# Attention, gated MLP, cosine MLP on one core: the order of both MLP layers written out by hand, with fixed leads for the weights

## The chip, the cores and the metric

The kernel runs on 1 core of a Trainium2 chip (trn2). Its engines are TensorE (PE), VectorE (DVE), ScalarE (ACT), GpSimd (POOL) and SyncE (SP), which here only issues DMAs. Each takes its instructions strictly in the order of its own list, and waits at an instruction whose inputs or buffers are not ready. The metric is device microseconds (us) of one launch, as the median of the runs.

## The reference, cut to what matters

```
attn[b,h] = softmax over keys in the query's hash bucket; out = attn @ v   # 2 x 8 heads, 768 x 64
x = attention out as 1536 tokens x 512
x = (sigmoid(x @ w_gate) * (x @ w_val)) @ w_out      # layer 1: 512 -> 1536 -> 512
h = x @ w_in                                          # layer 2: 512 -> 2048
y = (h * cos(h)) @ w_out2                             #          2048 -> 512
```

Weights arrive as float64, passed as pairs of 32-bit words.

## The kernel before, in words

Every fp32 product is made of three TensorE passes: each operand is split into a high part (rounded) and a low part (the rest), and high x high, high x low and low x high are added up in PSUM.

Attention comes first, in an order written out by hand. It writes its result, split, into `xy[c]`, where c = 0, 1, 2 are three groups of 512 tokens. The last heads finish c = 1 and c = 2.

The layers work in *items*. `("in", l, f, c)` is the first product of layer l for the f-th slice of 128 hidden columns and token group c: 24 matmuls of 512 columns in layer 1 (gate tile `pg` and value tile `pv`), 12 in layer 2 (`ph`). `("out", l, f, c)` multiplies the hidden slice into the output accumulators: 12 matmuls. Layer 1 has 12 slices and layer 2 has 16. For c = 0 the output item of a slice follows its three input items; those for c = 1 and c = 2 come in one long row at the end of the layer. So a *block* of layer 1 is 3 x 24 + 12 = 84 matmuls, one of layer 2 is 3 x 12 + 12 = 48, and layer 2 as a whole is 1152.

After an input item of layer 2 comes a chain that takes turns on two engines: ACT makes `n` (rounded phase), DVE makes `r`, ACT makes the sine in place in `r`, DVE makes `g`. Before the output item `g` has to be split by `gsplit`: ACT writes `gh`, DVE writes `gl`. In layer 1 the chain is a sigmoid on ACT and one product on DVE.

Each weight tile goes through three steps. `load_raw` puts 512 KB of float64 words into a `raw` buffer (SP queue). `convert` makes an fp32 tile `w_..`, of which there are 6 (`NEARLY`): `wp` on ACT, then `wl`, `wl`, `w` on DVE (L151 to L165). `wsplit` makes the high part on ACT (`ih`, `zh`, `gh`, `vh`, `oh`, L123) and the low part mostly on POOL (`il`, `zl`, ..., L124). The letters are g, v, o for layer 1 (gate, value, out) and i, z for layer 2 (in, out).

In both layers a scheduler decides the order on each engine before the kernel is built: it takes what is ready by its own estimate, with the order of the program as priority. The weights' three steps may therefore run far ahead, until the `raw` buffers (4) or the fp32 tiles (6) are full.

Of the kernel before, what the change touches and what calls it, by code (L numbers as in the profile page):

```python
# [9 lines left out]
F32 = mybir.dt.float32  # L10
# [29 lines left out]
def lsh_attention_glu_moe_cos_moe(  # L40
# [26 lines left out]

    const = ctx.enter_context(tc.tile_pool(name="const", bufs=1))

    wraw = ctx.enter_context(tc.tile_pool(name="wraw", bufs=4))  # L70
    NEARLY = 6

    ident = const.tile([P, P], F32, tag="ident", name="ident")
# [102 lines left out]


    def layer_items(l, F):
        items = [("in", l, 0, 0), ("in", l, 1, 0), ("in", l, 0, 1), ("in", l, 0, 2), ("in", l, 1, 1)]
        items += [("out", l, 0, 0), ("in", l, 1, 2), ("out", l, 1, 0)]  # L180
        for f in range(2, F):
            items += [("in", l, f, c) for c in range(NC)] + [("out", l, f, 0)]
        for f in range(F - 2):
            items += [("out", l, f, c) for c in range(1, NC)]
        items += [("out", l, f, c) for c in range(1, NC) for f in (F - 2, F - 1)]
        return items
# [7 lines left out]
            return [(nm, f, 0) for nm in ("gv" if l == 1 else "i")]  # L194
        return [("o" if l == 1 else "z", f, int(c > 0))]

    order = list(dict.fromkeys(kk for it in items for kk in weights_of(it)))
    done = 0
    def convert_to(n):
        nonlocal done  # L200
        while done < min(n, len(order)):
            load_to(done + 4)
            convert(order[done])
            done += 1

# [9 lines left out]
    def attention():  # L215
        with ExitStack() as st:
# [324 lines left out]
            with tc.manual_schedule(  # L541
                engines={
                    mybir.EngineType.PE,
                    mybir.EngineType.Activation,
                    mybir.EngineType.DVE,
                    mybir.EngineType.Pool,
                    mybir.EngineType.SP,
                }
            ):
                for t0 in (0, 3):  # L550
                    load(0, "q", t0, t0 + 3)
                    load(0, "k", t0, t0 + 3, eng=nc.scalar)
                constants()
                for g in range(2):
                    nc.sync.dma_start(pj[D * g : D * g + D, :], proj)
                nc.sync.dma_start(bcode, srow)
                load(1, "q")
                load(1, "k")
                load(0, "v")
                load(2, "k")  # L560
                load(2, "q")
                bit_weights()
                evac = [trans(0, half, fast=True) for half in range(2)]
                for fn in evac:
# [12 lines left out]
                coef(0)  # L577
                late.extend(bits(1, half) for half in range(2))
                for g in range(NG + LAG + 2):
                    wa, wb = 2 * (g - LAG), 2 * (g - LAG) + 1  # L580
                    fin = (wb - 2) // T if 0 <= wb - 2 < NW and (wb - 2) % T == T - 1 else None

                    def finish_group():
                        fin_act(fin)
                        if fin % 4 == 3:
                            at(g + SUM_AT, lambda u=fin: fin_sum(u))
                            at(g + HIGH_AT, lambda u=fin: fin_hi(u))
                            at(g + LOW_AT, lambda u=fin: fin_lo(u))

                    def early_weights():  # L590
                        if g == WL:
                            load_to(4)
                        if g in WC:
                            convert_to(1 + WC.index(g))
                            load_to(done + 4)

                    live_a, live_b, live_g = 0 <= wa < NW, 0 <= wb < NW, g < NG
                    ops = {
                        "PVb": (0 <= wb - 2 < NW, lambda: pv(wb - 2)),
                        "FIN": (fin is not None, finish_group),  # L600
                        "Tb": (live_b, lambda: ptrans(wb)),
                        "LOa": (live_a, lambda: plo(wa)),
                        "EXP": (live_g, lambda: expo(g)),
                        "PVa": (live_a and fin is None, lambda: pv(wa)),
                        "MIN": (g + 1 < NG, lambda: rowmax(g + 1)),
                        "HIb": (live_b, lambda: phi(wb)),
                        "Ta": (0 <= wa + 2 < NW, lambda: ptrans(wa + 2)),
                        "GRD": (live_g, lambda: guard(g)),
                        "COEF": (g + 1 < NG, lambda: coef(g + 1)),
                        "LOb": (live_b, lambda: plo(wb)),  # L610
                        "RCP": (live_g, lambda: recip(g)),
                        "NRM": (live_g, lambda: norm(g)),
                        "LATE": (True, run_late),
                        "W": (True, early_weights),
                        "S": (g + 2 < NG, lambda: scores(g + 2)),
                        "PVaF": (live_a and fin is not None, lambda: pv(wa)),
                        "PREP": (True, lambda: run_todo(g)),
                        "HIa": (0 <= wa + 2 < NW, lambda: phi(wa + 2)),
                    }
                    for name in ORDER if g >= LAG - 1 else FILL:  # L620
                        on, fn = ops[name]
                        if on:
                            fn()
                for step in sorted(todo):
                    run_todo(step)


    def moe():
        with ExitStack() as st:
# [8 lines left out]

            def wsplit(key):
                nm, f, again = key  # L640
                h = wsp.tile([P, KT, P], F32R, tag=ROLE[nm] + "h", name=f"{nm}h{again}_{f}")
                lw = wsp.tile([P, KT, P], F32R, tag=ROLE[nm] + "l", name=f"{nm}l{again}_{f}")
# [19 lines left out]
            gf, gs = {}, {}  # L662

            def gsplit(l, f, c):
                gh = wk.tile([P, 512], F32R, tag="gh", name=f"gh{l}_{c}_{f}", bufs=4)
                gl = wk.tile([P, 512], F32R, tag="gl", name=f"gl{l}_{c}_{f}", bufs=4)
                split(gh, gl, gf.pop((l, f, c)), nc.vector)
                gs[l, f, c] = gh, gl

# [8 lines left out]
                nc.vector.tensor_tensor(out=g, in0=pv_, in1=sg, op=ALU.mult)  # L678
                gf[1, f, c] = g

            def cos_in(c, f):
                ph = ps_h.tile([P, 512], F32, tag="h", name=f"ph{c}_{f}")
                proj_in(ph, c, ("i", f, 0))

# [4 lines left out]
                nc.vector.scalar_tensor_tensor(  # L689
                    out=r, in0=ph, scalar=INV2PI, in1=n, op0=ALU.mult, op1=ALU.subtract  # L690
                )
                nc.scalar.activation(r, r, AF.Sin, bias=halfpi, scale=TWOPI)
                g = gtile(2, f, c)
                nc.vector.tensor_tensor(out=g, in0=ph, in1=r, op=ALU.mult)
# [34 lines left out]
            def layer_out2(c, f):  # L729
# [3 lines left out]
                for t in range(4):  # L733
# [11 lines left out]
                        )  # L745
                        n += 1
                    if f == F2 - 1:
                        o = wk2.tile([P, 512], F32, tag="o", name=f"o{c}_{t}", bufs=3)
                        (nc.scalar.copy if t % 2 else nc.vector.tensor_copy)(o, acc[c, t])
                        b, tt = divmod(4 * c + t, T)  # L750
                        nc.sync.dma_start(
                            out.rearrange("(b p t) e -> b t p e", b=B, t=T)[b, tt], o
                        )


            ready = 0

            def ready_to(key):
                nonlocal ready
                while ready <= order.index(key):  # L760
                    convert_to(ready + 1)
                    wsplit(order[ready])
                    ready += 1
                    convert_to(min(ready + NEARLY - 2, len(order)))

            for key in weights_of(items[0]):
                ready_to(key)
            for n, (kind, l, f, c) in enumerate(items):
                late = kind == "out" and c > 0
                for it in items[n + 1 : n + (3 if late else 4)]:  # L770
                    for key in weights_of(it):
                        ready_to(key)
                for it in items[n + 1 : n + 3]:
                    if it[0] == "out" and it[1:] in gf:
                        gsplit(*it[1:])
                if kind == "in":
                    (glu_in if l == 1 else cos_in)(c, f)
                else:
                    (layer_out1 if l == 1 else layer_out2)(c, f)


    attention()
    moe()
# [41 lines left out]
```

## Time and profile before

| | |
|---|---|
| runs | 838.13, 838.14, 839.99 us; median 838.14 |
| profiled execution | 839.28 us; its span in the trace 837.1 us |
| PE busy | 804.0 us, 96% of the span |
| DVE busy | 579.6 us, 69% |
| ACT busy | 472.2 us, 56% |
| POOL busy | 317.9 us, 38% |

The span runs from the first to the last instruction of the trace; 2.2 us of the execution lie around it. Matmuls overlap one another in the trace, so PE is read by the distance between the starts of matmuls and not by its busy share.

### The profile page before, as it was taken

The page shows a single profiled execution, that of the slowest core. Times are in us where ns is not written, and L with a number is a line of the kernel's source. Part 1 is how long each engine was busy: PE and PEld are TensorE (multiplying, and loading weights), DVE is VectorE, ACT ScalarE, POOL GpSimd, SP SyncE. Part 2 cuts the span into 40 slices and gives each one's busy share as a digit, 9 for nine tenths or more (in the row PEclk, how much of TensorE's full clock was granted, in tenths as well). Part 3 has the DMA queues.
Part 4 walks back from the last instruction along what each step waited for, and adds up shares of the span by engine and source line. Part 5 has one row for each costly group of instructions (what it writes and reads, how often), then busy time and mean ns, then how long its engine had stood idle before and what let it go on. Part 6 is the DMA issues. An engine that isn't in the chain of part 4 may idle for free.

```text
span 837.1 us, 12085 instructions
## 1 busy us (share of the span) xinstructions
PE 804.0 (96%) x3984; PEld 673.9 (80%) x3984; DVE 579.6 (69%) x1157; ACT 472.2 (56%) x896; POOL 317.9 (38%) x315
## 2 busy tenths in 40 slices
PE   7999999999988999999999999998999999999997
PEld 5899899989976888888888888887777777778886
DVE  7999999999999664444444366876766766675422
ACT  5899899988986432333332244474555556564322
POOL 5688878878645222222222013212222222112221
PEclk9999999999999999999999999999999999999999
DMA  7666567575616433222222013323222322323002
GB/s 177 149 157 161 134 159 185 131 169 134 186 45 195 151 101 101 86 91 86 91 76 75 26 53 122 128 76 101 91 80 81 101 76 76 101 101 102 0 1 100
DMA packets 69069, 89.05 MB, mean 106 GB/s; under 512 B 29520, under 2 KB 52048, under 8 KB 69008
## 3 DMA queue, kind: packets, MB, share of 16 engines
q1 hardware_dynamic: 68208, 88.10, 36.8%
q8 instruction: 31, 0.51, 0.3%
q10 hardware_dynamic: 800, 0.20, 0.1%
q14 instruction: 30, 0.25, 0.1%
HBM read 59.77 MB, written 3.15 MB: 75 GB/s over the span
## 4 chain that ended last, share of the span: by engine, by line
PE 63%; issue 12%; DVE 11%; ACT 5%; POOL 5%; DMA 4%; SPq 0%; DVEq 0%; POOLq 0%; ACTq 0%
PE a L739 13%; PE pv L652 11%; PE pg L652 11%; PE a L712 10%; PE ph L652 5%; PE t L435 4%; DVE pl L445 2%; PE o L455 2%; PE o L456 2%; PE s L383 2%; PE s L386 2%; ACT p L409 1%; POOL il L124 1%; DMA e<-e 1%; POOL ef L478 1%
## 5 line engine op out<-in xcount | busy, mean ns | idle before, releaser
L124 DVE TENSOR_TENSOR gl<-g,gh 128x512 fp32r<-128x512 f32 x84 | 65.8, 789 | 76.5 <-ACT gh L123 75.6
L652 PE MATMUL ph<-xy,ih 128*128 128x512 f32 x384 | 118.2, 389 | 0.0
L409 ACT ACTIVATE p<-s,cb 128x768 f32<-128x768 f32 x96 | 96.2, 1002 | 13.3 <-DVE cb L395 6.5
L440 ACT CAST ph<-t 128x384 fp32r<-128x384 f32 x192 | 90.8, 486 | 16.1 <-PE t L435 12.2
L435 PE MATMUL t<-ident,p 128*128 128x128 f32 x576 | 94.7, 273 | 3.4 <-DVE pl L445 3.2
L445 DVE TENSOR_TENSOR pl<-t,ph 128x384 fp32r<-128x384 f32 x192 | 96.4, 540 | 1.8 <-ACT ph L440 0.8
L426 POOL TENSOR_SCALAR p<-p,r 128x768 f32<-128x768 f32 x96 | 87.0, 908 | 26.6 <-DVE r L422 12.5
L652 PE MATMUL pg<-xy,gh 128*128 128x512 f32 x288 | 89.6, 391 | 2.7 <-ACT xy L494 2.2
L390 DVE TENSOR_REDUCE mm<-s 128x1 f32<-128x768 f32 x96 | 90.7, 945 | 0.5 <-PE s L386 0.5
L652 PE MATMUL pv<-xy,vh 128*128 128x512 f32 x288 | 89.9, 393 | 0.8 <-ACT vh L123 0.8
L124 POOL TENSOR_TENSOR zl<-w_z,zh 128x512 fp32r<-128x512 f32 x32 | 43.6, 1363 | 113.6 <-ACT zh L123 113.6
L739 PE MATMUL a<-zh,gh 128*128 128x512 f32 x192 | 76.4, 398 | 10.8 <-ACT gh L123 10.6
L435 PEld LDWEIGHTS t<-ident,p 128*128 128x128 f32 x576 | 73.7, 140 | 14.5 <-DVE pl L445 7.1
L652 PEld LDWEIGHTS ph<-xy,ih 128*128 128x128 f32 x384 | 72.1, 188 | 15.0
L455 PE MATMUL o<-ph,vs 128*128 128x384 f32 x192 | 80.5, 419 | 1.3 <-ACT e L464 1.3
L123 ACT CAST gh<-g 128x512 fp32r<-128x512 f32 x84 | 51.3, 615 | 49.9 <-PE a L739 43.7
L739 PE MATMUL a<-zh,gl 128*128 128x512 f32 x192 | 76.3, 397 | 0.0
L739 PE MATMUL a<-zl,gh 128*128 128x512 f32 x192 | 74.9, 390 | 0.0
L652 PE MATMUL ph<-xy,il 128*128 128x512 f32 x192 | 74.7, 389 | 0.0
L124 POOL TENSOR_TENSOR ol<-w_o,oh 128x512 fp32r<-128x512 f32 x24 | 34.3, 1431 | 105.9 <-ACT oh L123 105.9
L383 PE MATMUL s<-k,q 96*128 96x384 f32 x192 | 69.4, 361 | 2.0 <-ACT p L409 1.3
L456 PE MATMUL o<-pl,vs 128*128 128x384 f32 x192 | 65.3, 340 | 2.9 <-DVE pl L445 2.9
(107 smaller groups left out, 1771.3 us busy)
## 6 DMA issues: line engine op xcount, KB each, us to landing
raw_z<-in_moe_w_out SPq DMA_DIRECT2D x32, 512.0 KB, 3.3
raw_o<-in_moe_w_out SPq DMA_DIRECT2D x24, 512.0 KB, 3.3
q<-x SPq DMA_DIRECT2D x45, 192.0 KB, 3.1
k<-x SPq DMA_DIRECT2D x45, 192.0 KB, 3.5
raw_i<-in_moe_w_in SPq DMA_DIRECT2D x16, 512.0 KB, 3.7
raw_g<-in_moe_w_gate SPq DMA_DIRECT2D x12, 512.0 KB, 3.6
raw_v<-in_moe_w_val SPq DMA_DIRECT2D x12, 512.0 KB, 3.8
nv<-in_v SPq DMA_DIRECT2D x8, 384.0 KB, 3.4
```

What stands on the lines that cost most here:

```text
L124: sub.tensor_tensor(out=dst_l, in0=src, in1=dst_h.bitcast(F32), op=ALU.subtract)
L383: nc.tensor.matmul(o, hh["q2"][0:96, t, :], hh["k2"][0:96, sl, :], start=True, stop=False)
L390: nc.vector.tensor_reduce(mm[:, g % NM, 1:2], s_t[g], axis=AX.XY, op=ALU.min)
L409: nc.scalar.activation(pt, s_t.pop(g), AF.Exp, bias=cb[:, 1:2], scale=cb[:, 0:1], accum_out=sm)
L426: nc.gpsimd.tensor_scalar(out=pt, in0=pt, scalar1=r_t.pop(g), scalar2=1.0, op0=ALU.mult, op1=ALU.mult)
L435: nc.tensor.transpose(pt[:, i, :], pv_[:, j * P : (j + 1) * P], ident)
L440: nc.scalar.copy(ph, pt_t[w])
L445: nc.vector.tensor_tensor(out=pl, in0=pt_t.pop(w), in1=ph_t[w].bitcast(F32), op=ALU.subtract)
L455: nc.tensor.matmul(o_t[u], vs[:, j, :], ph_t.pop(w), start=(j == 0), stop=False)
L652: nc.tensor.matmul(ps, w[:, kt, :], xy[c][:, hl, kt, :], start=(n == 0), stop=(n == 11))
L712: nc.tensor.matmul(acc[c, e], w[:, e, :], m, start=(f == 0 and n == 0), stop=(f == F1 - 1 and n == 2),)
L739: nc.tensor.matmul(acc[c, t], m[:, ts], w, start=(f == 0 and n == 0), stop=(f == F2 - 1 and n == 2),)
```

## The change

It puts both layers into a block in which the order of the program is the order on all five engines, as attention has it already. The steps of the weights are hung on items at fixed distances: a tile is converted `lead[0]` items and split `lead[1]` items ahead of the item that first uses it. In an input item of layer 2 all that is due there, the split of `g` among it, stands between `r` and the sine. There are three raw buffers where there were four, three of each `gh` and `gl` where there were four, three split tiles of the output weights where there were two, and four output tiles `o` where there were three. The order of the first eight items of layer 1 is another; that of layer 2 stays.

```diff
-    wraw = ctx.enter_context(tc.tile_pool(name="wraw", bufs=4))
+    wraw = ctx.enter_context(tc.tile_pool(name="wraw", bufs=3))
...
     def layer_items(l, F):
-        items = [("in", l, 0, 0), ("in", l, 1, 0), ("in", l, 0, 1), ("in", l, 0, 2), ("in", l, 1, 1)]
-        items += [("out", l, 0, 0), ("in", l, 1, 2), ("out", l, 1, 0)]
+        if l == 1:
+            items = [("in", l, 0, 0), ("in", l, 1, 0), ("out", l, 0, 0), ("in", l, 0, 1)]
+            items += [("out", l, 1, 0), ("in", l, 0, 2), ("in", l, 1, 1), ("in", l, 1, 2)]
...
+    def lead(key):
+        nm, f, again = key
+        if again:
+            return 4, 2
+        return {"g": (8, 4), "v": (7, 3), "i": (6, 3), "o": (5, 2), "z": (4, 3)}[nm]
+
+    order = sorted(use, key=lambda kk: use[kk] - lead(kk)[0])
...
-            load_to(done + 4)
+            load_to(done + 3)
...
-            def cos_in(c, f):
+            def cos_in(c, f, fill):
...
+                for fn in fill:
+                    fn()
                 nc.scalar.activation(r, r, AF.Sin, bias=halfpi, scale=TWOPI)
...
-                        o = wk2.tile([P, 512], F32, tag="o", name=f"o{c}_{t}", bufs=3)
+                        o = wk2.tile([P, 512], F32, tag="o", name=f"o{c}_{t}", bufs=4)
...
+            for n, (kind, l, f, c) in enumerate(items):
+                if kind == "out":
+                    m = items.index(("in", l, f, 0)) + 1 if c == 0 else n - 2
+                    due[m].append(lambda a=(l, f, c): gsplit(*a))
+            for kk in sorted(order, key=lambda kk: use[kk] - lead(kk)[1]):
+                due[split_at[kk]].append(lambda kk=kk: wsplit(kk))
+            for k, kk in enumerate(order[NEARLY:], NEARLY):
+                n = max(use[kk] - lead(kk)[0], split_at[order[k - NEARLY]])
+                due[n].append(lambda k=k: convert_to(k + 1))
+            with tc.manual_schedule(
+                engines={
...
+                convert_to(NEARLY)
+                for n, (kind, l, f, c) in enumerate(items):
+                    if (kind, l) == ("in", 2):
+                        cos_in(c, f, due[n])
+                        continue
+                    for fn in due[n]:
+                        fn()
```

ACT in the middle of layer 2, one block (slice 4). In the names `n20_4` is the phase of group c = 0 of slice 4 and `r0_4` its sine; the last number only tells buffers apart. Before:

```order
L151 ACTIVATE wp_i10_7561<-raw_i10_7424 128x512
L687 ACTIVATE n20_4_7242<-ph0_4_7229,quarter_63 128x512
L692 ACTIVATE r0_4_7244<-r0_4_7244,halfpi_62 128x512
L151 ACTIVATE wp_z10_7630<-raw_z10_7457 128x512
L123 CAST gh2_0_4_7262<-g2_0_4_7247 128x512
L687 ACTIVATE n21_4_7279<-ph1_4_7266,quarter_63 128x512
L692 ACTIVATE r1_4_7281<-r1_4_7281,halfpi_62 128x512
L687 ACTIVATE n22_4_7299<-ph2_4_7286,quarter_63 128x512
L123 CAST ih0_6_7351<-w_i6_7158 128x512
L692 ACTIVATE r2_4_7301<-r2_4_7301,halfpi_62 128x512
L123 CAST zh0_6_7420<-w_z6_7227 128x512
```

And now:

```order
L705 ACTIVATE n20_4_7211<-ph0_4_7198,quarter_63 128x512
L123 CAST zh0_4_7215<-w_z4_7184 128x512
L712 ACTIVATE r0_4_7213<-r0_4_7213,halfpi_62 128x512
L705 ACTIVATE n21_4_7235<-ph1_4_7222,quarter_63 128x512
L123 CAST gh2_0_4_7239<-g2_0_4_7220 128x512
L123 CAST ih0_5_7243<-w_i5_7172 128x512
L712 ACTIVATE r1_4_7237<-r1_4_7237,halfpi_62 128x512
L705 ACTIVATE n22_4_7263<-ph2_4_7250,quarter_63 128x512
L151 ACTIVATE wp_i6_7269<-raw_i6_7165 128x512
L712 ACTIVATE r2_4_7265<-r2_4_7265,halfpi_62 128x512
L151 ACTIVATE wp_z5_7281<-raw_z5_7177 128x512
```

The two conversions (`wp_i`, `wp_z`) left the place ahead of `gh2_0_4` for the end of the block; they are now for slices 6 and 5, where they were for slice 10. `gh2_0_4` stands directly behind the second phase.

PE where attention ends. `o31` is the last output tile of attention, `pg0_0` and `pv0_0` the first two tiles of layer 1. Before:

```order
L455 MATMUL o31_4382<-ph190_4412,vs15_3902 128x384
L652 MATMUL pv0_0_4528<-xy0_70,vh0_0_4488 128x512
L456 MATMUL o31_4382<-pl190_4420,vs15_3902 128x384
L455 MATMUL o31_4382<-ph191_4433,vs15_3902 128x384
L652 MATMUL pv0_0_4528<-xy0_70,vh0_0_4488 128x512
L652 MATMUL pv0_0_4528<-xy0_70,vl0_0_4489 128x512
```

And now:

```order
L472 MATMUL o31_4380<-pl191_4435,vs15_3902 128x384
L670 MATMUL pg0_0_4522<-xy0_70,gh0_0_4493 128x512 x2
L670 MATMUL pg0_0_4522<-xy0_70,gl0_0_4494 128x512
L670 MATMUL pg0_0_4522<-xy0_70,gh0_0_4493 128x512 x2
L670 MATMUL pg0_0_4522<-xy0_70,gl0_0_4494 128x512
```

No matmul of layer 1 stands any more between those of attention: all of them come behind its last one.

DVE at the same place, now. `pl191` is the last piece of attention; `w_v1`, `w_o0` and `w_o1` are the fourth to sixth converted weight tile, and `gl0_0` is the low part of the first gate tile, which the third matmul of layer 1 reads:

```order
L165 SCALAR_TENSOR_TENSOR w_v1_4427<-raw_v1_4343,wl_v1_4424 128x512
L461 TENSOR_TENSOR pl191_4435<-t191_4414,ph191_4431 128x384
L165 SCALAR_TENSOR_TENSOR w_o0_4482<-raw_o0_4372,wl_o0_4479 128x512
L153 TENSOR_SCALAR wl_o1_4488<-raw_o1_4404 128x512
L156 SCALAR_TENSOR_TENSOR wl_o1_4488<-wp_o1_4486,wl_o1_4488 128x512
L165 SCALAR_TENSOR_TENSOR w_o1_4491<-raw_o1_4404,wl_o1_4488 128x512
L124 TENSOR_TENSOR gl0_0_4494<-w_g0_4341,gh0_0_4493 128x512
```

Before, `gl0_0` stood in front of `w_v0`, between the pieces of attention; now it comes behind all six conversions.

## Rows read from the trace of the kernel before

**Rows 1.** The page: busy time, share and count of each engine.
```profile
PE 804.0 (96%) x3984; PEld 673.9 (80%) x3984; DVE 579.6 (69%) x1157; ACT 472.2 (56%) x896; POOL 317.9 (38%) x315
```

**Rows 2.** Timeline of PE (start us, us, instruction, count, [idle before <-releaser]).
```profile
312.65 0.39 PE L712 MATMUL a<-gh,oh 128*128 128x512 f32 x1
...
331.69 0.39 PE L712 MATMUL a<-gh,oh 128*128 128x512 f32 x1
...
552.61 0.61 PE L652 MATMUL ph<-xy,ih 128*128 128x512 f32 x2
...
832.28 0.39 PE L739 MATMUL a<-zh,gl 128*128 128x512 f32 x1
```

**Rows 3.** Timeline of PE: three output items of layer 2, first matmul.
```profile
585.05 0.50 PE L739 MATMUL a<-zh,gh 128*128 128x512 f32 x1 [2.36 <-ACT gh L123]
...
645.27 0.50 PE L739 MATMUL a<-zh,gh 128*128 128x512 f32 x1 [0.50 <-ACT gh L123]
...
657.51 0.50 PE L739 MATMUL a<-zh,gh 128*128 128x512 f32 x1 [0.80 <-ACT gh L123]
```

**Rows 4.** Waits, 585 to 748 us (us in total, times, longest us).
```profile
ACT wp_i L151 <- DMA raw_i<-in_moe_w_in: 15.0, 7, 2.3
DVE w_i L165 <- POOL il L124: 10.6, 9, 1.2
PE a L739 <- ACT gh L123: 10.6, 13, 2.4
```

**Rows 5.** Waits of the SP queue, 585 to 748 us.
```profile
SPq L136 <- DVE w_i L165: 59.4, 7, 9.6
```

**Rows 6.** Timeline of the SP queue in the block that ends at 648 us.
```profile
638.55 0.38 SPq L136 DMA_DIRECT2D raw_i<-in_moe_w_in  x1
```

**Rows 7.** Timeline of ACT in the same block.
```profile
642.38 0.67 ACT L151 ACTIVATE wp_i<-raw_i 128x512 f32<-128x512 f32 x1 [2.27 <-DMA raw_i<-in_moe_w_in]
643.12 0.72 ACT L692 ACTIVATE r<-r,halfpi 128x512 f32<-128x512 f32 x1
643.75 0.67 ACT L687 ACTIVATE n<-ph,quarter 128x512 int32<-128x512 f32 x1
644.60 0.62 ACT L123 CAST gh<-g 128x512 fp32r<-128x512 f32 x1 [0.18 <-DVE g L694]
```

**Rows 8.** The page's groups (count | busy us, mean ns of one | idle before, releaser).
```profile
L124 POOL TENSOR_TENSOR zl<-w_z,zh 128x512 fp32r<-128x512 f32 x32 | 43.6, 1363 | 113.6 <-ACT zh L123 113.6
L445 DVE TENSOR_TENSOR pl<-t,ph 128x384 fp32r<-128x384 f32 x192 | 96.4, 540 | 1.8 <-ACT ph L440 0.8
```

**Rows 9.** Windows, matmuls of L652 alone (us, PE busy (count), clock, DMA share, GB/s).
```profile
247.00:258.90 11.90, 6.87 (x26) 1.00 0.41 138
...
247.00:274.50 27.50, 19.53 (x72) 0.94 0.54 175
```

**Rows 10.** Timeline of PE where attention ends.
```profile
257.90 0.44 PE L456 MATMUL o<-pl,vs 128*128 128x384 f32 x1
...
268.62 0.50 PE L652 MATMUL pg<-xy,gh 128*128 128x512 f32 x1 [2.19 <-ACT xy L494]
...
274.56 0.63 PE L652 MATMUL pg<-xy,gh 128*128 128x512 f32 x2
```

**Rows 11.** Timeline of DVE and of POOL at the same place.
```profile
246.26 0.69 DVE L165 SCALAR_TENSOR_TENSOR w_g<-raw_g,wl_g 128x512 int32<-128x512 int32 x1
...
247.80 0.42 DVE L153 TENSOR_SCALAR wl_v<-raw_v 128x512 int32<-128x512 int32 x1
...
251.00 1.45 DVE L153 TENSOR_SCALAR wl_g<-raw_g 128x512 int32<-128x512 int32 x1
...
260.03 4.19 POOL L124 TENSOR_TENSOR ol<-w_o,oh 128x512 fp32r<-128x512 f32 x1 [7.86 <-ACT oh L123]
```

**Rows 12.** Windows of 1 us, PE (us, busy (count), granted clock, DMA share, GB/s).
```profile
270.00:271.00 1.00, 1.00 (x3) 0.50 0.00 0
```

**Rows 13.** Timeline of ACT at the end.
```profile
833.57 0.59 ACT L749 COPY o<-a 128x512 f32<-128x512 f32 x1 [1.63 <-DMA out_y<-o]
```

More of the change, by code (lines that the diff above doesn't have):

```diff
@@ L178, in layer_items @@
     def layer_items(l, F):
-        items = [("in", l, 0, 0), ("in", l, 1, 0), ("in", l, 0, 1), ("in", l, 0, 2), ("in", l, 1, 1)]
-        items += [("out", l, 0, 0), ("in", l, 1, 2), ("out", l, 1, 0)]
+        if l == 1:
+            items = [("in", l, 0, 0), ("in", l, 1, 0), ("out", l, 0, 0), ("in", l, 0, 1)]
+            items += [("out", l, 1, 0), ("in", l, 0, 2), ("in", l, 1, 1), ("in", l, 1, 2)]
+        else:
+            items = [("in", l, f, 0) for f in range(2)] + [("in", l, 0, 1), ("in", l, 0, 2)]
+            items += [("in", l, 1, 1), ("out", l, 0, 0), ("in", l, 1, 2), ("out", l, 1, 0)]
         for f in range(2, F):
@@ L195, in weights_of @@
         return [("o" if l == 1 else "z", f, int(c > 0))]
-    order = list(dict.fromkeys(kk for it in items for kk in weights_of(it)))
+    use = {}
+    for n, it in enumerate(items):
+        for kk in weights_of(it):
+            use.setdefault(kk, n)
+    def lead(key):
[4 more added lines that the diff above has]
+    order = sorted(use, key=lambda kk: use[kk] - lead(kk)[0])
     done = 0
@@ L591, in early_weights @@
                         if g == WL:
-                            load_to(4)
+                            load_to(3)
                         if g in WC:
                             convert_to(1 + WC.index(g))
-                            load_to(done + 4)
+                            load_to(done + 3)
                     live_a, live_b, live_g = 0 <= wa < NW, 0 <= wb < NW, g < NG
@@ L640, in wsplit @@
                 nm, f, again = key
-                h = wsp.tile([P, KT, P], F32R, tag=ROLE[nm] + "h", name=f"{nm}h{again}_{f}")
-                lw = wsp.tile([P, KT, P], F32R, tag=ROLE[nm] + "l", name=f"{nm}l{again}_{f}")
+                role = ROLE[nm]
+                nb = 3 if role == "c" else 2
+                h = wsp.tile([P, KT, P], F32R, tag=role + "h", name=f"{nm}h{again}_{f}", bufs=nb)
+                lw = wsp.tile([P, KT, P], F32R, tag=role + "l", name=f"{nm}l{again}_{f}", bufs=nb)
                 sub = nc.vector if key in (("g", 0, 0), ("g", 1, 0), ("v", 1, 0)) else nc.gpsimd
@@ L664, in gsplit @@
             def gsplit(l, f, c):
[L665 to L666 removed]
+                gh = wk.tile([P, 512], F32R, tag="gh", name=f"gh{l}_{c}_{f}", bufs=3)
+                gl = wk.tile([P, 512], F32R, tag="gl", name=f"gl{l}_{c}_{f}", bufs=3)
                 split(gh, gl, gf.pop((l, f, c)), nc.vector)
@@ L753, in layer_out2 @@
                         )
[L756 to L767, printed above, removed]
-            for n, (kind, l, f, c) in enumerate(items):
[L769 to L779, printed above, removed]
+            due = [[] for _ in items]
@@ new lines, in moe @@
+            split_at = {kk: max(use[kk] - lead(kk)[1], 0) for kk in order}
+            for n, (kind, l, f, c) in enumerate(items):
+                if kind == "out":
[5 more added lines that the diff above has]
+                n = max(use[kk] - lead(kk)[0], split_at[order[k - NEARLY]])
+                assert n <= split_at[kk]
+                due[n].append(lambda k=k: convert_to(k + 1))
@@ new lines, in moe @@
+            with tc.manual_schedule(
+                engines={
+                    mybir.EngineType.PE,
+                    mybir.EngineType.Activation,
+                    mybir.EngineType.DVE,
+                    mybir.EngineType.Pool,
+                    mybir.EngineType.SP,
+                }
+            ):
+                convert_to(NEARLY)
[5 more added lines that the diff above has]
+                        fn()
+                    if kind == "in":
+                        glu_in(c, f)
+                    else:
+                        (layer_out1 if l == 1 else layer_out2)(c, f)
```

## The prediction

> **What bounds the kernel now.** I read the page first: PE is busy 96% of the span, no other engine over 69% [rows 1], so the time is PE's work and the places where PE stands still. Busy time says little of a pipelined engine, so next the timeline of PE, by the distance between starts. In the middle of layer 1 one block of 84 matmuls takes 331.69 - 312.65 = 19.04 us [rows 2]: 0.2267 us each, with no idle mark. That is the pace of both layers, and their 2448 matmuls cost 554.9 us by it. What is left to win lies above this pace:
>
> - Layer 2 runs from 552.61 to the start of its last matmul at 832.28 [rows 2]: 279.67 us, where 1151 steps of 0.2267 make 260.9. So 18.7 us are lost in it.
> - From 274.56, when 72 matmuls of layer 1 are done [rows 9, 10], to 552.61 are 278.05 us for 1224 matmuls, which need 277.5: 0.6 us lost in layer 1.
> - 72 matmuls before 274.56 amount to a start at 274.56 - 72 x 0.2267 = 258.24 without any pause. I use this "effective start" to price the passage from attention to layer 1.
>
> Where the 18.7 us lie, the waits tell: between 585 and 748 us the only large wait of PE is that of the output matmuls for ACT's `gh`, 13 times and 10.6 us [rows 4]. Two neighbouring output items start 657.51 - 645.27 = 12.24 us apart, where 48 matmuls need 10.88 [rows 3]; so a block loses 1.36 us, idle time and the slower steps after it, and the first stop alone is 2.36 us.
>
> The timeline of ACT in one such block shows why `gh` is late. Behind the first phase `n` ACT stands idle for 2.27 us at `wp_i`, a conversion that nobody needs soon, until its raw tile lands at 642.38; only behind it come the sine, the next `n`, and `gh` at 644.60 [rows 7]. The load was issued at 638.55 [rows 6], 3.8 us before. It was issued so late because SP waits for a raw buffer, which DVE's conversions free (59.4 us of such waits for `w_i` alone) [rows 5], and DVE's conversions in turn wait for POOL to free one of the six fp32 tiles (10.6 us) [rows 4]. The conversions have run as far ahead as the buffers allow, and then each engine waits in line for the next one with the useful work queued behind it.
>
> **The change part by part.** *Layer 2, the order.* Let a block of PE begin at 0; inputs end at 2.7, 5.4 and 8.2, the output item at 10.9. I take 0.7 us for each instruction of ACT and DVE (0.62 to 0.72 on ACT in [rows 7]; 0.69 on DVE in [rows 11]). New order of ACT: `n0` 2.8 to 3.5, `zh` to 4.2, sine 4.2 to 4.9 (DVE has made `r` by then); DVE makes `g0` by 5.6. `n1` 5.5 to 6.2, then `gh` to 6.9. DVE: `r1` to 6.9, `gl` to 7.6. Both are ready before 8.2, when the output item asks for `gh`; `gl` it asks for two matmuls later. So the slack is 1.3 us for `gh` and 1.0 for `gl`, and the stop is gone. The rest of the block on ACT is `ih`, sine, `n2`, `wp_i`, sine, `wp_z`, over by 10.9, and nothing there stands in front of `gh` of this block. All in all 11 instructions of 0.7, or 7.7 of 10.9 us; DVE has 13, or 9.1. `il` and `zl` on POOL (1.36 us each for `zl` [rows 8]) have an item or more to spare. I take the whole 18.7 us: **-18.7**. Bounds: 0 and 18.7.
>
> *Three raw buffers.* Loads alternate i, z, i, z. With three buffers a load of `z` waits for the conversion of the `i` before it, which ends at 11 us in the block before, and is used at 10.1 in the next: 10 us for a load of 3.8. For `i` it is 17 us. Both are hidden by a whole block of matmuls. Three `gh`/`gl` pairs: in the long rows of output items a pair takes the place of the one three items back, so `gh` and `gl` (1.4 us) have two items, 5.4 us. Both cost nothing as long as PE runs behind this cover; without it, see the second rival.
>
> *Layer 1.* Its ACT chain is short and the splits have two items or more; its 0.6 us goes: **-0.6** (bounds -0.6 and 0).
>
> *The end.* The last copy of ACT waits until 833.57 for the DMA that frees an output tile [rows 13]; the last matmul ends at 832.28 + 0.39 = 832.67 [rows 2]. With a fourth tile it starts at 832.75: **-0.8**, bounds 0 and -0.9.
>
> *The passage.* Before, 26 matmuls of layer 1 were done between the last ones of attention [rows 9], 5.9 us of work in gaps that were there anyway. Now all stand behind attention's last matmul. Against that, less work of the layers stands between attention's last pieces on ACT and DVE, and two stops go: `xy` of group 1 (2.19 us [rows 10]) now comes 12 matmuls later in PE's list, and the half clock that followed it [rows 12]. What is late next is `gl0_0`, which the third matmul needs and which stands on DVE behind all six conversions. `w_g0` ends at 246.95 [rows 11]; then come five conversions of 0.42 + 2 x 0.69 = 1.8 us, seven `pl` of 0.5 (0.54 each, [rows 8], a little less in a row), and `gl` itself: 246.95 + 9.0 + 3.5 + 0.7 = 260.15. Less the two matmuls ahead of it, the effective start is 259.7, which is 1.5 us later than 258.24: **+1.5**. Bounds: attention cannot end before DVE has done all but the last conversion and `gl`, about 257.6, hence -0.6 at best; at worst the 26 matmuls are lost in full, +5.9.
>
> Sum: -18.7 - 0.6 - 0.8 + 1.5 = -18.6. The profiled execution took 839.28 us, of which 837.1 are the span, so 820.7. The median of the runs is 1.14 us below it: 819.5. I write **820**.
>
> **The rivals.** *TensorE's clock falls in the passage.* Before, PE stood still for 2.19 us and once more, and then ran at 0.50, that is 1.2 GHz, for some 3 us [rows 10, 12]. Now PE is thinly loaded while attention ends, and then waits some 2 us for `gl0_0`. Against it: stops like the 2.36 us one [rows 3] between full blocks were followed by matmuls at full pace. Price: as much as it cost before, half of 3.4 us, 1.7: 821. The Trainium skill (TensorE: Matmul & The Clock Gate, section "Why this matters for your kernels") has the same rule, that gaps of idle TensorE put the clock back to half; this trace agrees after 268.62.
>
> *Too few buffers: slower.* The mechanism would be a raw tile that lands late in every block, with ACT waiting at `wp_i` in front of the sine. It has its place at 8.9 us in the block. The new list leaves ACT 2.9 us free between `wp_z` and the next `n0`, and `gh` 1.3 more, so a wait costs PE from 4.2 us on, and the kernel is slower from 4.2 + 1.36 = 5.6 us in each of 14 blocks; at 6.5 us it gives 839 + 14 x 0.9 = 852. For it speaks that there is one buffer less, and that DMA waits were on this chain; against it that the longest was 2.3 us [rows 4] and the loads now have 10 us. The Trainium skill (Perfetto Trace Analysis, section "Optimization Strategy") says that a gap which repeats on the busiest engine can mean too few buffers. This trace shows such a gap, but the buffers are full of tiles for five slices ahead, so I read it as order.
>
> *Half of the stops stay.* If DVE and POOL hold each other up (a `wl_g` of DVE took 1.45 us where another took 0.42, and an `ol` of POOL took 4.19 [rows 11]), `gl` could miss its 1.0 us. Half of 18.7 would give 829. Against it: in the new list `gl` has no conversion near it.
>
> *Nothing happens*: the passage costs its 5.9 us and most stops stay, within 0.3% of 838. I see no row for it.
>
> **How the numbers follow.** Forecast 0.57, clock 0.24, half 0.10, buffers 0.05, nothing 0.04. The range goes from the best bound of the passage, 839.28 - 20.7 - 1.14 = 817.4, less half a microsecond for scatter, 817, to the worst, 819.5 + 4.4 + 1.7 = 825.6; the likeliest alone 818 to 822. Runs of one kernel here lie up to 1.9 us apart, so 0.3% (2.5 us) is about what tells a change from none. Faster 0.91, same 0.04, slower 0.05.
>
> **What would show it.** Output items of layer 2 10.9 us apart and no wait of PE for `gh`; SP's loads of `raw_i` issued 10 us or more before `wp_i`, and no DMA wait of ACT there; 26 fewer matmuls of L670 before attention's last one, and PE waiting for DVE's `gl` once, near 260. The prediction is wrong if PE waits for `gh` or `gl` in each block, or if the effective start is beyond 262.

## The result and the profile after

The changed kernel takes 827.1 us (median of 4 runs, 826.57 to 828.79) beside 838.27 (838.13 to 839.99) of the kernel before: a ratio of 0.9861, 95% interval 0.9844 to 0.9877. It is faster, clear of the noise though by less than 2%: 11.2 us where 18 were forecast, and it lies above the range. The profiled execution took 826.57 us, with a span of 824.8 where before it was 837.1.

The timeline of PE after, at the same places as [rows 2, 3]: the last of layer 1's first slow steps, two output items of layer 2, layer 2's first matmul and last.

```profile
265.84 0.63 PE L670 MATMUL pv<-xy,vh 128*128 128x512 f32 x2
...
556.21 0.62 PE L670 MATMUL ph<-xy,ih 128*128 128x512 f32 x2
...
641.31 0.39 PE L759 MATMUL a<-zh,gh 128*128 128x512 f32 x1
...
652.19 0.39 PE L759 MATMUL a<-zh,gh 128*128 128x512 f32 x1
...
820.65 0.39 PE L759 MATMUL a<-zh,gl 128*128 128x512 f32 x1
```

The two output items are 652.19 - 641.31 = 10.88 us apart, the pace without a loss, where before it was 12.24 [rows 3], and neither has an idle mark. Layer 2 as a whole runs 820.65 - 556.21 = 264.44 us where 1151 steps of 0.22667 need 260.9: 3.5 us are lost, 18.8 before. Layer 1 loses nothing: its 1296 matmuls need 293.76 us, so layer 2's first matmul at 556.21 gives an effective start of 262.45, and the 15 matmuls that were done by 265.84 give 262.44.

| part of the span, us | before | after | difference | forecast |
|---|---|---|---|---|
| effective start of layer 1 | 258.24 | 262.45 | +4.2 | +1.5 |
| lost in layer 1 | 0.6 | 0.0 | -0.6 | -0.6 |
| lost in layer 2 | 18.8 | 3.5 | -15.2 | -18.7 |
| last matmul's start to the end of the span | 4.8 | 4.15 | -0.7 | -0.8 |
| sum | | | -12.3 | -18.6 |

So 2.7 us are missing in the passage and 3.5 in layer 2. The rest of the distance between 820 and 827.1 lies outside these rows: the forecast took the median 1.14 us below the profiled execution, and here it lies 0.5 above.

**Layer 2's middle.** The timeline of ACT in the block whose output item starts at 641.31 and which so began 36 matmuls, 8.16 us, earlier, at 633.15, beside [rows 7]:

```profile
636.13 0.69 ACT L705 ACTIVATE n<-ph,quarter 128x512 int32<-128x512 f32 x1 [2.71 <-PE ph L670]
636.71 0.61 ACT L123 CAST zh<-w_z 128x512 fp32r<-128x512 f32 x1
637.57 0.72 ACT L712 ACTIVATE r<-r,halfpi 128x512 f32<-128x512 f32 x1 [0.25 <-DVE r L707]
638.85 0.69 ACT L705 ACTIVATE n<-ph,quarter 128x512 int32<-128x512 f32 x1 [0.55 <-PE ph L670]
639.43 0.61 ACT L123 CAST gh<-g 128x512 fp32r<-128x512 f32 x1
```

ACT now waits for PE, no longer for a raw tile, and `gh` is done at 640.04, 6.9 us after the block began, as forecast; the output item asks for it at 8.2. The sign for the loads came true too: loads run three tiles ahead, so the `raw_i` that SP issues at 625.74 is the one that `wp_i` reads at 642.15, 16.4 us later, and neither ACT nor DVE has a wait for a raw tile between 560 and 820 us.

**Layer 2's last block.** PE's idle marks where the first pass ends and the second begins, and DVE, POOL and ACT in front of the first of them:

```profile
728.91 0.50 PE L759 MATMUL a<-zh,gh 128*128 128x512 f32 x1 [0.41 <-ACT gh L123]
...
732.69 0.50 PE L759 MATMUL a<-zl,gh 128*128 128x512 f32 x1 [0.25 <-POOL zl L124]
...
735.17 0.50 PE L759 MATMUL a<-zh,gh 128*128 128x512 f32 x1 [0.37 <-DVE g L714]
...
736.46 0.47 PE L759 MATMUL a<-zh,gh 128*128 128x512 f32 x1 [0.33 <-DVE o L769]
```

```profile
724.50 1.52 DVE L153 TENSOR_SCALAR wl_z<-raw_z 128x512 int32<-128x512 int32 x1
726.12 0.69 DVE L156 SCALAR_TENSOR_TENSOR wl_z<-wp_z,wl_z 128x512 int32<-128x512 int32 x1
726.92 0.69 DVE L165 SCALAR_TENSOR_TENSOR w_z<-raw_z,wl_z 128x512 int32<-128x512 int32 x1
727.53 0.68 DVE L714 TENSOR_TENSOR g<-ph,r 128x512 f32<-128x512 f32 x1
...
724.44 1.29 POOL L124 TENSOR_TENSOR zl<-w_z,zh 128x512 fp32r<-128x512 f32 x1 [6.27 <-ACT zh L123]
```

```profile
728.24 0.62 ACT L123 CAST gh<-g 128x512 fp32r<-128x512 f32 x1 [1.67 <-DVE g L714]
```

Of the regular blocks, this one alone has a conversion of `z` for the second pass on DVE between `r` and `g` of its first input item, and the first step of that conversion takes 1.52 us beside POOL's `zl`, where 64 of the 96 such steps take 0.42. `g` comes at 727.53, `gh` ends at 728.86, 8.7 us into the block and so 0.5 too late. Another such stop of 0.47 us, for `zl` of slice 1, comes at 576.11. With the slower steps after each, these marks make up the 3.5 us: 0.8 at 576.11 and 2.7 at the change of pass.

**The passage.** PE, DVE and POOL where attention ends, beside [rows 10, 11], and then the windows of PE (the last three columns are granted clock, DMA share and GB/s):

```profile
256.05 0.69 PE L472 MATMUL o<-pl,vs 128*128 128x384 f32 x1 [2.34 <-DVE pl L461]
256.66 1.22 PE L670 MATMUL pg<-xy,gh 128*128 128x512 f32 x2
260.18 0.80 PE L670 MATMUL pg<-xy,gl 128*128 128x512 f32 x1 [2.30 <-DVE gl L124]
```

```profile
258.37 1.75 DVE L124 TENSOR_TENSOR gl<-w_g,gh 128x512 fp32r<-128x512 f32 x1
...
257.85 1.73 POOL L124 TENSOR_TENSOR vl<-w_v,vh 128x512 fp32r<-128x512 f32 x1 [14.55 <-ACT vh L123]
```

```profile
255.00:255.50 0.50, 0.00 (x0) 1.00 0.00 0
255.50:256.00 0.50, 0.00 (x0) 0.52 0.00 0
...
265.50:266.00 0.50, 0.50 (x3) 0.74 0.00 0
```

The wait for `gl0_0` is there once, and ends at 260.18, within 0.03 us of the 260.15 that the forecast worked out. But PE had stood still for 2.34 us before it as well, for attention's last `pl`: before, 26 matmuls of layer 1 lay in such gaps [rows 9], and the list by hand has none of them there. The clock fell to 0.50 (1.2 GHz) inside that first stop and came back at 265.7. At full pace the 16th matmul would have started at 260.18 + 13 x 0.2267 = 263.13; it started at 265.84, so the clock cost 2.7 us.

### The profile page after: what moved, and what is told of

The parts are those of the page before. It is cut to its first block, busy times and chain, and to the rows that moved or that the text cites. A ratio compares the mean times of both kernels' runs of the same rounds, so it can differ in the third digit from the quotient of the medians.

```text
span 824.8 us, 12075 instructions
## 1 busy us (share of the span) xinstructions
PE 798.6 (97%) x3984; PEld 676.8 (82%) x3984; DVE 609.1 (74%) x1157; ACT 469.1 (57%) x896; POOL 312.3 (38%) x315
## 3 DMA queue, kind: packets, MB, share of 16 engines
HBM read 59.77 MB, written 3.15 MB: 76 GB/s over the span
## 4 chain that ended last, share of the span: by engine, by line
PE 81%; DVE 9%; issue 3%; ACT 3%; DMA 2%; POOL 1%; SPq 0%; DVEq 0%; POOLq 0%; ACTq 0%
PE a L759 15%; PE ph L670 14%; PE pg L670 12%; PE pv L670 12%; PE a L732 12%; PE t L451 5%; PE o L471 2%; PE o L472 2%; PE s L399 2%; PE s L402 2%; DVE pl L461 2%; PE pb L360 1%; DVE cb L411 1%; DMA e<-e 1%; ACT p L425 1%
## 5 line engine op out<-in xcount | busy, mean ns | idle before, releaser
L124 POOL TENSOR_TENSOR zl<-w_z,zh 128x512 fp32r<-128x512 f32 x32 | 41.8, 1307 | 169.5 <-ACT zh L123 169.5
L696 DVE TENSOR_TENSOR g<-pv,sg 128x512 f32<-128x512 f32 x36 | 24.8, 690 | 99.3 <-PE pv L670 99.3
L694 ACT ACTIVATE sg<-pg 128x512 f32<-128x512 f32 x36 | 21.3, 592 | 117.8 <-PE pg L670 117.8
L670 PEld LDWEIGHTS ph<-xy,ih 128*128 128x128 f32 x384 | 72.0, 188 | 15.1
L124 DVE TENSOR_TENSOR gl<-g,gh 128x512 fp32r<-128x512 f32 x84 | 59.8, 714 | 32.7 <-ACT gh L123 30.5
```

Of the source, the lines that this page charges most:

```text
L124: sub.tensor_tensor(out=dst_l, in0=src, in1=dst_h.bitcast(F32), op=ALU.subtract)
L670: nc.tensor.matmul(ps, w[:, kt, :], xy[c][:, hl, kt, :], start=(n == 0), stop=(n == 11))
```

## The experiments

In the table, "passage" is the distance from one row of attention that all kernels share (the matmul of `o<-pl` with about 1.3 us of idle time in front of it, at 247.06 in the changed kernel and 247.47 before) to layer 1's effective start with layer 1's own losses in it. It is counted from that row because attention itself lay up to 1.7 us earlier or later from one execution to the next. "Lost" is layer 2's time above 260.9 us. The kernels were measured in several groups, each with the kernel before beside it, so kernels of different groups are compared by their ratios; where the intervals overlap, the times do not tell them apart, and only the traces (one execution each) can.

| kernel | median us | ratio to before (95%) | passage | lost in layer 2 |
|---|---|---|---|---|
| before | 838 to 840 | | 11.4 | 18.8 |
| changed | 827.1 | 0.9861 (0.9844-0.9877) | 15.4 | 3.5 |
| two early splits | 822.98 | 0.9806 (0.9780-0.9832) | 11.5 | 3.5 |
| four raw buffers, three output tiles | 830.39 | 0.9892 (0.9872-0.9913) | 15.65 | 5.8 |
| order left to the scheduler | 845.17 | 1.0070 (1.0049-1.0091) | 12.0 | 25.0 |
| conversions as early as they can | 848.08 | 1.0100 (1.0075-1.0126) | 20.9 | 16.7 |
| four early splits | 823.93 | 0.9817 (0.9797-0.9838) | 11.8 | 3.6 |
| the same with the old list | 817.95 | 0.9746 (0.9725-0.9767) | 5.9 | 3.6 |
| four early splits, z one item earlier | 824.32 | 0.9819 (0.9801-0.9838) | 12.3 | 3.15 |
| first low halves on DVE | 826.14 | 0.9841 (0.9823-0.9859) | 14.0 | 3.6 |
| old list alone | 826.92 | 0.9861 (0.9832-0.9890) | 15.1 | 3.6 |
| old list, four early splits, chosen leads | 815.94 | 0.9730 (0.9706-0.9755) | 5.9 | 2.4 |

**Two early splits.** The first two splits of layer 1 go ahead of conversions 5 and 6:

```diff
-                due[split_at[kk]].append(lambda kk=kk: wsplit(kk))
+                if kk not in (("g", 0, 0), ("v", 0, 0)):
+                    due[split_at[kk]].append(lambda kk=kk: wsplit(kk))
...
+                for kk in (("g", 0, 0), ("v", 0, 0)):
+                    wsplit(kk)
                 convert_to(NEARLY)
```

> The first two weights of layer 1 (gate and value of slice 0) are split ahead of conversions 5 and 6 instead of behind all six; the rest is as in the changed kernel. Theory (PE's gaps at attention's end, with nothing to fill them, cost 2.7 us of half clock on top of the wait): the order now puts 24 matmuls of layer 1 between attention's last ones, so no stop over 1.5 us is left, the granted clock stays 1.00 there, and the effective start moves from 262.45 to 256 to 258.5: 820.5 to 823.5 us. Rival (attention's own last stop for DVE's pl drops the clock anyway): a stretch at 0.50 stays and the effective start is 259.5 to 261: 824 to 826. Second rival (the passage is not where the time is): 826.5 to 828. Layer 2 should lose the same 3.5 us as in the changed kernel.

Measured 822.98 us. On PE, 24 matmuls of layer 1 now lie among attention's last ones, and no stop is left until the second gate tile, whose `gl` still stands behind conversion 6. Its row on PE, and PE's windows around it:

```profile
261.64 0.79 PE L670 MATMUL pg<-xy,gl 128*128 128x512 f32 x1 [2.67 <-DVE gl L124]
```

```profile
258.00:259.00 1.00, 0.73 (x2) 1.00 0.79 167
259.00:260.00 1.00, 0.00 (x0) 1.00 1.03 369
260.00:261.00 1.00, 0.00 (x0) 0.83 0.90 231
261.00:262.00 1.00, 0.36 (x1) 0.50 0.97 232
```

The time fits the theory, but its claim that no stop would be left does not hold. The clock held through attention's end, where there was no stop, and fell inside the one that remained. The passage is 3.9 us shorter, layer 2 unchanged.

**Four raw buffers.** Raw buffers 3 to 4, loads four ahead; output tiles 4 to 3 for the space.

```diff
-    wraw = ctx.enter_context(tc.tile_pool(name="wraw", bufs=3))
+    wraw = ctx.enter_context(tc.tile_pool(name="wraw", bufs=4))
...
-            load_to(done + 3)
+            load_to(done + 4)
...
-                        o = wk2.tile([P, 512], F32, tag="o", name=f"o{c}_{t}", bufs=4)
+                        o = wk2.tile([P, 512], F32, tag="o", name=f"o{c}_{t}", bufs=3)
```

> A fourth raw buffer, paid for with the fourth output tile (which goes back to three); loads run four ahead as before. Theory (three raw buffers cost nothing that counts): ACT's waits for raw_o near 253 and 254 (0.75 and 1.94 us) go, but gl of the first weight is held by DVE's own row of conversions, so it is at most 0.7 us earlier; layers 1 and 2 lose what they lost; the end is 0 to 0.8 us longer: 826.0 to 828. Rival (the third buffer's late loads are what makes the passage long): effective start 2 us or more earlier, 823 to 825.5.

Measured 830.39: the fourth buffer buys nothing (passage 15.65, against 15.4), and the fourth output tile is worth more than either theory had. The waits of ACT between 700 and 760 us:

```profile
ACT o L769 <- DMA out_y<-o: 5.2, 1, 5.2
```

With three tiles ACT waits 5.2 us for an output to leave in the middle of layer 2, where the first pass ends, and layer 2 loses 5.8 us instead of 3.5; the end is 0.7 us longer, close to the 0.8 forecast for this tile. Two things changed at once here; a fourth raw buffer with all four output tiles was not run.

**The order left to the scheduler.** The manual schedule around the two layers is taken away; list, leads and buffers stay.

```diff
-            with tc.manual_schedule(
-                engines={
...
-            ):
+            if True:
```

> The changed kernel with the order of the two layers left to the scheduler again: same program order, same leads, same buffers. Theory (the written order on each engine removed layer 2's stops): layer 2 loses 10 to 19 us again, the passage is 3 to 5 us shorter since matmuls may again lie among attention's last ones: 831 to 840. Rival (the leads alone, by setting when each conversion may start, removed the stops): layer 2 loses 5 us or less and the time is 820 to 826.

Measured 845.17, above the theory's range: the passage is 3.4 us shorter, as it said, but layer 2 loses 25.0 us, more than before. ACT waits for raw tiles again, as in [rows 4]; between 560 and 760 us:

```profile
ACT wp_z L151 <- DMA raw_z<-in_moe_w_out: 24.6, 22, 1.9
ACT wp_i L151 <- DMA raw_i<-in_moe_w_in: 6.9, 6, 1.2
```

So the leads alone do not remove the stops: the scheduler takes conversions forward from where the program has them. Counted from the n-th `wp_i` to the n-th `ih` on ACT, a tile of `i` is converted 55 to 68 us ahead of its split from the fifth on, where the changed kernel has 8.7 us. Why layer 2 loses more than before is open; there is one raw buffer less, and the same with four was not run.

**Conversions as early as they can.** By hand still, but each conversion directly behind the split that frees its fp32 tile.

```diff
-            return 4, 2
-        return {"g": (8, 4), "v": (7, 3), "i": (6, 3), "o": (5, 2), "z": (4, 3)}[nm]
+            return 99, 2
+        return {"g": (99, 4), "v": (99, 3), "i": (99, 3), "o": (99, 2), "z": (99, 3)}[nm]
...
-                n = max(use[kk] - lead(kk)[0], split_at[order[k - NEARLY]])
+                n = max(use[kk] - lead(kk)[0], max(split_at[kj] for kj in order[: k - NEARLY + 1]))
```

> The changed kernel, order still given by hand, but each conversion stands as early as the six fp32 tiles allow (behind the split that frees its tile) instead of at its fixed lead. Theory (stops come from conversions ahead of their need, whose waits for raw tiles and fp32 tiles stand in line in front of useful work): ACT waits at wp_i or wp_z for DMA again in most blocks of layer 2, and layer 2 loses 8 to 20 us: 831 to 845. Rival (it is the place given to sine, gh and gl by hand that counts, whatever the lead): layer 2 loses under 5 us, 825 to 829.

Measured 848.08, 3 us above the theory's range. Layer 2 loses 16.7 us, the size that the theory gave, by another way than it said: ACT does not wait for raw tiles. The passage is 5.5 us longer as well, which the theory did not have: `gl` of the first gate tile comes later (a stop of 3.25 us for it), and the first output item stops 2.27 us for `gh` at 277.56, with the clock at 0.50 again behind it. One block on DVE, ACT and PE, as each block is:

```profile
647.89 1.52 DVE L153 TENSOR_SCALAR wl_z<-raw_z 128x512 int32<-128x512 int32 x1
...
650.93 0.69 DVE L714 TENSOR_TENSOR g<-ph,r 128x512 f32<-128x512 f32 x1
...
651.64 0.62 ACT L123 CAST gh<-g 128x512 fp32r<-128x512 f32 x1 [1.67 <-DVE g L714]
...
652.32 0.50 PE L759 MATMUL a<-zh,gh 128*128 128x512 f32 x1 [0.41 <-ACT gh L123]
```

This is the changed kernel's last block again, number for number: a conversion of `z` between the first `r` and its `g`, its first step 1.52 us long, `gh` 0.41 us late for PE. Output items are 11.90 us apart (652.32 and 640.42), 1.02 above the pace, 14 times. So the hand order does not help by itself either; what counts is that no conversion stands in front of the `g` that the next output item needs. In front of the third item's `g` one does no harm: the changed kernel has one of `i` there in each middle block.

**Four early splits.** As with two, for `g` and `v` of slices 0 and 1.

```diff
-                due[split_at[kk]].append(lambda kk=kk: wsplit(kk))
+                if kk not in (("g", 0, 0), ("v", 0, 0), ("g", 1, 0), ("v", 1, 0)):
+                    due[split_at[kk]].append(lambda kk=kk: wsplit(kk))
...
+                for kk in (("g", 0, 0), ("v", 0, 0), ("g", 1, 0), ("v", 1, 0)):
+                    wsplit(kk)
                 convert_to(NEARLY)
```

> As the run with the two early splits, but the splits of the first two gate and value tiles (four in all) stand ahead of conversions 5 and 6. With two early splits one stop of 2.67 us was left, for the low half of the second gate tile, and the clock fell to 0.50 behind it. Theory (stops of this kind are what lowers the clock; where none is left the clock stays): no stop over 1 us between 250 and 266, no stretch at 0.50, effective start 253 to 255: 817 to 820 us. What may be late next is xy of group 1, asked for by the 61st matmul near 267 and ready at 267.6: a wait of up to 1 us. Rival (the clock falls for another reason, such as attention's mix of small matmuls): a stretch at 0.50 near 260 stays and the time is 821 to 823.

Measured 823.93: the stop for the second gate tile is gone, and one of 5.15 us has come, at the third item of the new list, `out(0,0)`. DVE and PE there:

```profile
263.52 2.10 DVE L156 SCALAR_TENSOR_TENSOR wl_g<-wp_g,wl_g 128x512 int32<-128x512 int32 x1
265.66 1.21 DVE L165 SCALAR_TENSOR_TENSOR w_g<-raw_g,wl_g 128x512 int32<-128x512 int32 x1
266.79 0.68 DVE L696 TENSOR_TENSOR g<-pv,sg 128x512 f32<-128x512 f32 x1
...
268.17 0.80 PE L732 MATMUL a<-gh,oh 128*128 128x512 f32 x1 [5.15 <-ACT gh L123]
```

`g` of the first slice waits behind a conversion that is slowed while POOL adds up `ef` and splits `xy`, and `out(0,0)` stands too early in the list for that. The clock falls at the end of this stop (0.51 from 268 to 270). Neither theory had this place, and the time lies above both.

**The same with the old list.** Layer 1's first eight items as in the kernel before, so that `out(0,0)` is sixth and not third.

```diff
-        if l == 1:
-            items = [("in", l, 0, 0), ("in", l, 1, 0), ("out", l, 0, 0), ("in", l, 0, 1)]
-            items += [("out", l, 1, 0), ("in", l, 0, 2), ("in", l, 1, 1), ("in", l, 1, 2)]
-        else:
-            items = [("in", l, f, 0) for f in range(2)] + [("in", l, 0, 1), ("in", l, 0, 2)]
-            items += [("in", l, 1, 1), ("out", l, 0, 0), ("in", l, 1, 2), ("out", l, 1, 0)]
+        items = [("in", l, f, 0) for f in range(2)] + [("in", l, 0, 1), ("in", l, 0, 2)]
+        items += [("in", l, 1, 1), ("out", l, 0, 0), ("in", l, 1, 2), ("out", l, 1, 0)]
```

> As the run with four early splits, but layer 1's first eight items in the order of the kernel before, so that group 1's xy is asked for by the 49th matmul and not the 61st. Theory (the new list is worth something only when layer 1 starts early): PE stops 2 to 4 us for xy near 264.5 and runs at half clock behind it: 2.5 to 6 us slower than the run with four early splits, 820 to 825. Rival (xy comes early enough in either list): within 1 us of it.

Measured 817.95, 6 us less than with the new list, the opposite of what the theory said. The largest stop that is left is the one for `xy`, and the clock stays up; PE's row and its windows:

```profile
265.82 0.49 PE L666 MATMUL pg<-xy,gh 128*128 128x512 f32 x1 [0.54 <-POOL xy L510]
```

```profile
264.00:266.00 2.00, 1.40 (x6) 1.00 0.48 170
266.00:268.00 2.00, 2.00 (x9) 1.00 0.00 0
```

**z one item earlier**, with four early splits and the new list.

```diff
-            return 4, 2
-        return {"g": (8, 4), "v": (7, 3), "i": (6, 3), "o": (5, 2), "z": (4, 3)}[nm]
+            return 5, 2
+        return {"g": (8, 4), "v": (7, 3), "i": (6, 3), "o": (5, 2), "z": (5, 3)}[nm]
```

> Four early splits, and conversions of z one item earlier: those of the second pass 5 items ahead instead of 4, those of the first pass 5 instead of 4. Theory (layer 2's last 3.5 us come from a conversion that stands between a slice's first r and its g on DVE, in the fill of the block's first input item, where it also meets POOL's zl and takes 1.5 us instead of 0.4): layer 2 loses 1 us or less, and the time is 2 to 3 us below that of four early splits: 814.5 to 817.5. Rival (the last block is short of engine time wherever the conversion stands): layer 2 loses 2.5 us or more, no difference.

Measured 824.32; layer 2 loses 3.15 instead of 3.6. The stop for `gh` is gone, but a conversion now stands on DVE in front of the copies of `o`, and PE waits 1.2 us for these at 733.5. The rival comes nearer: one lead for all moves the stop.

**First low halves on DVE.** `vl` and `ol` of slice 0 move from POOL to DVE.

```diff
-                sub = nc.vector if key in (("g", 0, 0), ("g", 1, 0), ("v", 1, 0)) else nc.gpsimd
+                sub = nc.vector if key in (("g", 0, 0), ("v", 0, 0), ("o", 0, 0), ("g", 1, 0), ("v", 1, 0)) else nc.gpsimd
```

> The changed kernel with the low halves of the first value and output tiles (vl, ol of slice 0) on DVE instead of POOL, behind gl of the first gate tile. Theory (DVE's gl took 1.75 us there instead of 0.69 because POOL worked at the same time): gl takes 0.7 us, PE's third matmul of layer 1 starts 0.9 to 1.1 us earlier, and the time is 0.5 to 1.5 us less: 825.5 to 826.6. Rival (POOL has no hand in it): gl takes 1.7 us again and the time is 827 to 828.5, since DVE has two instructions more.

Measured 826.14, and on DVE:

```profile
259.38 0.68 DVE L124 TENSOR_TENSOR gl<-w_g,gh 128x512 fp32r<-128x512 f32 x1
```

0.68 us instead of 1.75: the work of POOL beside it was the cause of `gl`'s length. The passage is 1.4 us shorter in the trace; the interval of the time overlaps that of the changed kernel.

**The old list alone**, by the same edit of the list, in the changed kernel.

> The changed kernel with layer 1's first eight items in the order of the kernel before, nothing else. Theory (in the changed kernel layer 1 starts so late that neither list makes PE wait: xy of group 1 is there at 267.8 and would be asked for at 273): within 0.3% of the changed kernel, 826 to 828.5. Rival (the new list removed a stop for xy, as the forecast had it): a stop of 2 us or more for xy near 273 and 829 to 831.

Measured 826.92: no difference, and PE has no stop for `xy`. The new list bought nothing, since layer 1 starts too late there for either list to matter.

**Chosen leads**, on top of the old list and four early splits:

```diff
-            return 4, 2
+            return (5 if f < 2 else 4), 2
+        if (nm, f) == ("z", 1):
+            return 5, 4
```

> Four early splits and the old list of layer 1 (817.95 us as it stood), and in layer 2: the second pass's conversions of z for slices 0 and 1 five items ahead, the others four as in the changed kernel; z of slice 1 converted five and split four items ahead. Moving all of them by one item took away the stop for gh but put a conversion in front of DVE's copies of o at the change from the first to the second pass. Theory (the conversions near that change and the first zl are all that layer 2 still loses): layer 2 loses 0.3 to 1.0 us instead of 3.6, nothing else moves, and the time is 814.5 to 816. Rival (another wait takes their place there again): layer 2 loses 2.5 us or more, 817 to 818.5.

Measured 815.94. The change of pass now costs 0.9 us, but at the beginning of layer 2 a wait of 0.63 us for `il` took the place of that for `zl`: 2.4 lost in all, between the two theories. The time lies in the theory's range, but its interval overlaps that of the run without the chosen leads, so the gain over that run is read from layer 2 alone. Against the changed kernel, both by their ratios to before, this is 1.3% less.

## Why the prediction was wrong

- *The diagnosis of layer 2* was right for the scheduler's order: conversions ahead of their need stood in front of the sine and of `gh`. Left to the scheduler again they wait for raw tiles again, and layer 2 loses 25.0 us. Taken early by hand (about 35 us ahead of their splits) they bring 16.7 us back too, but by their place in front of `g` and without a wait for a raw tile, so being early is not the cause by itself. In the middle blocks the forecast's step times hold to 0.3 us, and the end of `gh` to less than 0.1.
- *"I take the whole 18.7 us"* is the first step that failed, by 3.5. I worked out one regular block and gave its result to all. The two ends of the layer are other blocks: in the last one the lead of the second pass puts a conversion in front of `g`, in the first one `zl` is late. The bounds, 0 and 18.7, held it; the value was taken at their end.
- *The passage, "+1.5"* is the second, by 2.7. The time of `gl0_0` was right to 0.03 us, by luck, with two errors that cancel: DVE's row ended 1.1 us sooner than I had added up (0.4 of it because attention lay earlier in this execution), and `gl` took 1.75 us instead of 0.7. What failed is that the clock was left to a rival. That rival (1.7 us, chance 0.24) happened at 2.7. Its argument against itself, that stops between full blocks had been followed by full pace, came from another place than the one in question: here there were two stops with few matmuls between them.
- I had also named the sign that the prediction is wrong, an effective start beyond 262; it is 262.45.
- *Three raw buffers cost nothing*: the changed kernel has no wait for a raw tile in layer 2, and the run with four is no better in the passage. *Layer 1's 0.6 goes*: it did. *The end, -0.8*: measured 0.7. In the order by hand the fourth output tile saves 2.2 us more where the passes change, which I did not see.
- *Two stops for `xy` go because of the new list*: they went, but not because of the list. With the old list alone nothing changes, and once layer 1 starts in time the new list costs 6 us.
- The rival *Half of the stops stay*, by which DVE and POOL hold each other up, had 0.10. Its mechanism is at work, in the last block and for `gl0_0`, but not in each block.

## What to carry to other kernels

Price the first and the last round of a loop by themselves: an order that is right for the middle can put a conversion in front of the critical step at the ends, and each loss there also costs slower steps behind it. When an order by hand is drawn up phase by phase, look for work that the scheduler had let run across the boundary; here taking 26 matmuls out of attention's gaps left a passage of 15.4 us where it had been 11.4 with the two stops for `xy`, and giving them back (with the item list of before) brought 9 us. A wait that is removed uncovers the next one, so a reordered list has to be tried again after every such step.

## What the runs showed of the hardware

- DVE is held up by POOL's elementwise work beside it. The shift of `L153` takes 0.42 us alone and 1.52 beside a `zl` of 1.29; `gl` takes 0.69 alone and 1.75 beside `vl` of 1.73, and 0.68 again when that work of POOL is taken away. The Trainium skill (GPSIMD Engine Reference, section "1. Specifications") lists the SBUF interfaces of that engine as shared with VectorE, with contention for DVE instructions in a two-port mode or with two SBUF inputs. The rows of `gl`, which has two, agree; whether `L153`, which has one, runs in such a mode no run shows.
- The price is what is left of POOL's instruction when DVE's starts. In the changed kernel 49 DVE instructions of `L153`, `L156`, `L165` and `L124` start while POOL runs a subtraction of `L124`: all 33 of `L153` end 0.28 or 0.29 us behind POOL's, and 15 of the 16 others, all with two inputs, 0.55 behind it. One that starts first keeps its time: the `L165` at 257.76, 0.09 us ahead of `vl`, took 0.69, and `vl` took 1.73 where `zl` took 1.29. The kernel before has exceptions: five that start inside its `ol` of 4.19 us [rows 11] are not held up.
- The granted clock fell to 0.50 inside or shortly behind a stop of 1.9 to 5.2 us at the passage in each kernel that had one, and stayed at 1.00 from 250 to 275 us in the two kernels where none there was over 0.6 (old list with four early splits, with and without the chosen leads). Length alone does not tell: before, a stop of 2.36 us in layer 2 [rows 3] was followed by full pace, and with the order left to the scheduler two stops of the same 1.47 us, at 636.23 and 649.26, had a clock of 1.00 (638 to 647) and of 0.51 (652 to 654) behind them. What decides between such stops is not shown.
